# Two units of the third transform factor at once at a quad's end, and one tile for partial sums and output

## The chip, the cores and the metric

The kernel runs on one core of one Trainium2 chip. The metric is the device time of one execution in microseconds (us). The reports call the engines PE (TensorE matmul), PEld (TensorE weight load), DVE (VectorE), ACT (ScalarE), POOL (GpSimd) and SP (SyncE, which issues most DMAs here; "SPq" is its queue).

## The reference, cut to what matters

```python
# x: (8, 3008, 256), filt: (1505, 256), w_in: (256, 2048), w_out: (2048, 256), all float32 in effect
Y = np.fft.rfft(x, axis=1) * (filt_r + 1j * filt_i)[None]
x = np.fft.irfft(Y, n=3008, axis=1).reshape(24064, 256)
h = x @ w_in
g = np.where(h > 0.0, h, np.exp(np.minimum(h, 0.0)) - 1.0)
out = g @ w_out
```

A circular convolution along the sequence, by the frequency domain, and then a dense layer, an ELU and a second dense layer on every row.

## The kernel before

**Two parts side by side.** Each of the 8 batches goes through a transform in factors (3008 = 47 x 64) and then through the dense layers. While the dense layers of batch b - 1 run, pieces of the transform of batch b are placed between their steps. The work of a batch in the dense layers is 6 units (m = 0 to 5) of 512 rows (448 for m = 0) in four quads (q = 0 to 3, a quarter of the 2048 hidden columns each): 24 quads a batch, 192 in all. A *period* is 24 quads, and "quad 22" is the one with index 22 in it.

**A quad.** The two dense layers use a product scheme of seven multiplications in place of eight on blocks of 2 x 2. `up_steps` gives seven steps of the first layer (two matmuls each, `mm`, L583) into a PSUM bank taken from `banks`, with the sums on VectorE (L591), copies on ScalarE (L594) and the ELU on both (L600, L601, L605). `down_steps` gives seven steps of the second layer for the quad before it (L665), which add up in four banks `po0` to `po3` over four quads. The loop at the end (L1047 on) writes the order out by hand: U and D in the strings are the next up and down step, the first string of a quad, then the *places* 2 and 3 inside it, place 0 in the quad's middle, the second string, and place 1 at its end. A quad whose index is in `opens` starts with a down step: its strings are "DUUDUDDU" and "DUUDUD", else "UUDUDDU" and "DUUDUDD". `at(quad, place, ...)` puts a piece of other work there; every engine runs what it is given in this order, and the DMA queue of SP too.

**PSUM.** Eight banks: `po0` to `po3`, and four in the list `banks`, taken from its front and put back at its end. A quad's up steps hold two to three of these at a time.

**The pieces of the transform** of a batch, with their quads in the period: `a_unit` (first factor, L237; ends of quads 0, 3 and 4), `b_unit` (second factor, L388; ends of 6, 10, 14, 18), the products with the filter on VectorE, `bi_unit` (second factor back, L460, with ACT's copies at L463; ends of 9, 13, 17, 21), and `y_write` (L471), which writes a part of the DRAM tile `yd` right after. Each of these takes all four banks. Then the third factor, `n_unit` (L522 to L543), once for each unit m: `tn_read` (L483) loads its table, `y_read` (L494) loads rows of all of `yd` into a tile `t4` with two DMAs of 256 KB, one for each half of the partitions; 32 small matmuls of 64x64 shape (L535; 64 records in the trace) fill two banks, and ScalarE copies these to `y0` and `y1` (L542). `n_sums` (L545) makes the remaining operands of the up steps from them on VectorE, into `yb` and `yt`. Its places are written out at the end: `n_unit` stands in the middle (place 0) of quads 23, 25, 29, 32, 36 and 40, counted from the start of the period before the unit's own dense layers, whose first quad is 24; modulo 24 these are 23, 1, 5, 8, 12 and 16. `y_read` is placed two quads ahead in the middle of a quad, for m = 0 at the end of quad 21, behind the last `y_write`. Units 0 and 1 of batch 0 have another form, `n_whole`, with full-size matmuls.

**The end of a unit.** In the last quad's down steps ScalarE copies `po0` and `po1` to two tiles `k0` and `k1` of the pool `kp` (L670), VectorE joins them with `po2` and `po3` into `c` (L681, partly in `c_unit` in the next quad), and `o_unit` in the quad after that transposes `c` into `o`, a tile of a pool `op` of its own (L706), and issues 16 stores to the output (L715; 20 for m = 0). The last unit ends in `o_last`.

Pools give out buffers in turn; an instruction that writes to a buffer waits for the readers of its old content. SP's DMAs use eight semaphores in turn, and each waits for the DMA that used its semaphore before.

Of the kernel before, what the change touches and what calls it, by code (L numbers as in the profile page):

```python
# [11 lines left out]
FP32 = mybir.dt.float32  # L12
# [14 lines left out]
P = 128  # L27
# [106 lines left out]
def kernel(  # L134
# [371 lines left out]
    def n_whole(b, m):  # L506
        t, w, h = t4s.pop((b, m)), tns.pop((b, m)).rearrange("p i (k t) -> p i k t", k=2), half(m)
        rows = []
        for dh in range(2):
            y = yp.tile([P, 2, 256], FP32, tag="y%d" % dh, name="y%d" % dh)[:, :, 0:h]  # L510
            k, ps = bank("psn", (P, 2, 256))
            for q, i in enumerate(order(m)):
                nc.tensor.matmul(ps[:, :, ts(q, 64)], t[:, i - 4 * m, ds(dh * P, P)], w[:, i - 4 * m], start=True, stop=True)
            nc.scalar.activation(out=y, in_=ps[:, :, 0:h], func=AXT.Copy)
            banks.append(k)
            rows += [y[:, 0], y[:, 1]]
        b11, b12, b21, b22 = rows
        t = yp.tile([P, 2, 256], FP32, tag="yb", name="yb")[:, :, 0:h]
        t2 = yp.tile([P, 256], FP32, tag="yt", name="yt")[:, 0:h]
        ys[b, m] = {1: b11, 2: b21, 3: b22, 4: t[:, 1], 5: t[:, 0], 6: t2, 7: b12}  # L520

    def n_unit(b, m):  # L522
        if whole(b, m):
            return n_whole(b, m)
        t, w, h = t4s.pop((b, m)), tns.pop((b, m)), half(m)
        ps = [bank("psn", (P, 2, 256)) for _ in range(2)]
        for q, i in enumerate(order(m)):
            for dh in range(2):
                for c in range(2):
                    for (_, p), r in zip(ps, HALVES):  # L530
                        o = p[ts(c, 64), dh, ts(q, 64)]
                        if last(b, m):
                            o = p[ts(c, 64), dh, q:]
                            o = bass.AP(tensor=o.tensor, offset=o.offset, ap=[list(o.ap[0]), [131 - 2 * q, 2], [4, 32]])
                        nc.tensor.matmul(o, t[r, i - 4 * m, ds(dh * P + 64 * c, 64)],  # L535
                                         w[r, i - 4 * m, :], start=True, stop=True)
        even, odd, both = (yp.tile([P, 2, 256], FP32, tag=n, name=n)[:, :, 0:h] for n in ("y0", "y1", "yb"))
        t2 = yp.tile([P, 256], FP32, tag="yt", name="yt")[:, 0:h]
        ys[b, m] = {1: both[:, 0], 2: both[:, 1], 3: even[:, 1], 4: odd[:, 1], 5: odd[:, 0], 6: t2, 7: even[:, 0],
                    "even": even, "odd": odd, "both": both}  # L540
        for t, (k, p) in zip((even, odd), ps):
            nc.scalar.activation(out=t, in_=p[:, :, 0:h], func=AXT.Copy)  # L542
            banks.append(k)  # L543

    def n_sums(b, m, *parts):  # L545
        if whole(b, m):
            b11, b21, b22, t4, t1, t2, b12 = (ys[b, m][k] for k in range(1, 8))
            for o, x, y in ((t1, b12, b11), (b12, b22, b12), (t2, b22, t1), (t4, b21, t2)):
                nc.vector.tensor_tensor(out=o, in0=x, in1=y, op=ALU.subtract)
            return  # L550
        even, odd, both, t2 = (ys[b, m][k] for k in ("even", "odd", "both", 6))
        steps = ((both, odd, -0.5, even, ALU.add), (even[:, 1], odd[:, 1], 0.5, even[:, 1], ALU.add),
                 (t2, even[:, 1], 1.0, odd[:, 0], ALU.subtract), (even[:, 0], t2, 1.0, both[:, 0], ALU.subtract),
                 (odd[:, 1], both[:, 1], 1.0, t2, ALU.subtract))
        for i in parts or range(5):
            o, x, c, y, op = steps[i]
            if c == 1.0:
                nc.vector.tensor_tensor(out=o, in0=x, in1=y, op=op)
            else:
                nc.vector.scalar_tensor_tensor(out=o, in0=x, scalar=c, in1=y, op0=ALU.mult, op1=op)  # L560
# [92 lines left out]
    def down_steps(b, m, q):  # L653
        h = half(m)
        g = g_of.pop((b, m, q))
        if q == 0:
            po_of[b, m] = [psO.tile([P, 2, 256], FP32, tag="po%d" % i, name="po%d" % i) for i in range(4)]
        po = po_of[b, m]
        k = {}

        def step(n):
            i, u = PLACE[n]
            for a in range(2):

                nc.tensor.matmul(po[i][:, u, 0:h], w_out[q][:, COMBO[n], a, :], g[n][:, a, :],  # L665
                                 start=q == 0 and a == 0 and n in (1, 3, 6, 4), stop=True, skip_group_check=True)
            if q == 3 and n == 7:
                for i in range(2):
                    t = k[i] = kp.tile([P, 2, 256], FP32, tag="k%d" % i, name="k%d" % i)
                    nc.scalar.activation(out=t[:, :, 0:h], in_=po[i][:, :, 0:h], func=AXT.Copy)  # L670

        def tail():
            if q != 3:
                return
            p1, p5 = (k[0][:, u, 0:h] for u in range(2))
            p35, p7 = (k[1][:, u, 0:h] for u in range(2))
            c = kp.tile([P, 2, 512], FP32, tag="c", name="c")
            (c11, c12), (c21, c22) = ((c[:, i, 0:h], c[:, i, h:2 * h]) for i in range(2))

            def add(o, i0, i1):  # L680
                nc.vector.tensor_tensor(out=o, in0=i0, in1=i1, op=ALU.add)  # L681

            add(p35, p35, p5)
            add(c12, po[2][:, 1, 0:h], p1)
            add(c11, po[2][:, 0, 0:h], p1)
            rest = [(p7, p7, c12), (c21, po[3][:, 0, 0:h], p7), (c12, c12, p35), (c22, p7, p5)]
            cs_[b, m] = c, lambda i: [add(*r) for r in rest[i:i + 2]]

        return [(lambda n=n: step(n)) for n in DOWNS], tail


# [6 lines left out]
    def o_unit(b, m):  # L698
        c, join = cs_.pop((b, m))
        join(2)  # L700
        o = op.tile([P, 16, 2, 32], FP32, tag="o", name="o")
        if last(b, m):
            return o_last(b, m, c, o.rearrange("p (k f j) e s -> p k f (j e s)", k=2, f=2))
        n = 7 if m == 0 else 8
        for k in range(2):
            nc.vector.transpose(out=o.rearrange("p (j k) e s -> p j k e s", k=2)[:, 0:n, k],  # L706
                                in_=c[:, :, k * half(m):(k + 1) * half(m)].rearrange("p e (j s) -> p j e s", s=32))

        o = o.rearrange("p (u f k) e s -> p u f k (e s)", u=4, f=2)
        for k in range(2):  # L710
            for u, w, i in ((0, 3, 1), (3, 1, 0)) if m == 0 else ((0, 4, 4 * m),):
                for f in range(1 if i == 0 else 2):
                    n1 = N1 - i if f else i
                    for a in range(4):
                        nc.sync.dma_start(raw(out, b * N + n1 + 32 * N1 * k,  # L715
                                                   [[N1 * D, 32], [-D if f else D, w], [1, 64]], 64 * a),
                                               o[ts(a, 32), u:u + w, f, k])
# [121 lines left out]
    with tc.manual_schedule():  # L839


        with tc.tile_pool(name="boot", bufs=1) as bp:
# [24 lines left out]
            def places(m, e, c):  # L867
                wtmp.append((m.bitcast(U32), e.bitcast(U32), c[:, 0], c[:, 1]))

            def flat(t):  # L870
                return t.rearrange("p a b -> p (a b)")

            places(*(kp.tile([P, 512], FP32, tag=t, name=n) for t, n in (("k0", "wm"), ("k1", "we"))),
                   kp.tile([P, 2, 512], FP32, tag="c", name="wfl"))
            places(*(flat(sdp.tile([P, 2, D], FP32, tag="sd", name=n)) for n in ("wm", "we")),
                   t1p.tile([P, XC, D], FP32, tag="t1", name="wfl").rearrange("p (a b) d -> p a (b d)", a=2))
# [86 lines left out]
        yp = pool("yp", 2)  # L963
        gp = pool("gp", 2)
        ep = pool("ep", 2)
        op = pool("op", 1)
        n_unit(0, 0)
        n_sums(0, 0)

# [23 lines left out]
        for b in range(B):  # L993
            t = (b - 1) * PER
            if b > 0:
# [15 lines left out]
                for g in range(0, NG, 2):  # L1011
# [14 lines left out]
                    at(s + 3, 2, im_sums, b, g)  # L1026
                    at(s + 3, 1, bi_unit, b, g)
                    at(s + 3, 1, y_write, b, g)
            for m, s in enumerate((23, 25, 29, 32, 36, 40)):
                if b > 0 or m > 0:  # L1030
                    at(t + s - 2, 0, tn_read, b, m)
                    at(t + s - 2, 1 if m == 0 else 0, y_read, b, m)
                    if b == 0 and m == 1:
                        at(t + s, 1, n_unit, b, m)
                        at(t + s, 1, n_sums, b, m)
                    else:
                        at(t + s, 0, n_unit, b, m)
                        for place, *parts in (((t + s, 0), 0, 1, 2), ((t + s + 1, 2), 3, 4)) if m == 0 else (
                                ((t + s, 0), 0, 1), ((t + s, 1), 2, 3, 4)) if m < 3 else (((t + s + 2, 2),),):
                            at(*place, n_sums, b, m, *parts)  # L1040
                if b == 0 and m == 1:
                    at(1, 1, w_join, 13)
                at(t + PER + 4 * m + 5, 0, c_unit, b, m)
# [58 lines left out]
```

## Time and profile before

| | us |
|---|---|
| median of 3 runs | 2559.9 (2559.11 to 2561.76) |
| the profiled execution's own time | 2560.57 |
| its span, first to last instruction | 2558.6 |
| PE busy at L665 (down steps) | 1317.6 |
| PE busy at L583 (up steps), the five largest groups | 388.4 + 380.3 + 193.8 + 193.8 + 185.9 |
| PE busy at L535 (third factor) | 53.4 |
| DVE, ACT busy in all | 2066.1, 1544.9 |
| granted TensorE clock, mean | 0.997 |

The page gives busy times, the chain of work that ended last, and groups of instructions by source line. The timeline lists instructions in order of time, neighbours of one kind merged (start, length, engine, line, tiles, count; in brackets the engine's idle time ahead of them). Matmul records overlap: the start of the next one tells when the engine went on. The list of waits names who waited for whom, with the total, the count and the longest. The table by windows has, for each stretch, its length, the busy time and count of each engine, and at the end the granted clock, the DMA engines' share and GB/s.

### The profile page before, as it was taken

The numbers are of one execution on the slowest core, as the hardware profiler recorded it, in microseconds if no ns is written. First come the engines' busy times: TensorE is split into PE (matmuls) and PEld (weight loads), VectorE is DVE, ScalarE is ACT, GpSimd is POOL, SyncE is SP. The second block draws the span as 40 slices with busy tenths as digits, with TensorE's granted clock in tenths as the row PEclk, the third lists the DMA queues.
The fourth block names the chain that finished last, engine by engine and source line by source line (L and its number), as shares of the span: only waits on it lengthen the run. The fifth ranks groups of instructions, "written<-read, shape, count | busy, mean of one in ns | idle before, by whom it ended". The sixth has DMA issues, their size and how long they took to land.

```text
span 2558.6 us, 43997 instructions
## 1 busy us (share of the span) xinstructions
PE 2522.3 (99%) x16690; PEld 2164.8 (85%) x16690; DVE 2066.1 (81%) x3577; ACT 1544.9 (60%) x2716; POOL 160.2 (6%) x315
## 2 busy tenths in 40 slices
PE   6999999999999999999999999999999999999999
PEld 4788889888898888988889888888888888898888
DVE  6978887788878888788887888778897788876766
ACT  7765556655566565665566656565656655555555
POOL 5001000010000000000000000000100011000000
PEclk9999999999999999999999999999999999999999
DMA  9672213522133231433215231343213322110010
GB/s 281 178 189 65 62 39 81 130 67 69 44 102 100 67 69 40 121 82 72 57 44 150 64 80 36 77 122 81 60 41 85 84 63 69 36 46 18 19 28 17
DMA packets 228295, 200.62 MB, mean 78 GB/s; under 512 B 127174, under 2 KB 200406, under 8 KB 228084
## 3 DMA queue, kind: packets, MB, share of 16 engines
q1 hardware_dynamic: 213588, 166.93, 26.6%
q0 software_dynamic: 14000, 30.44, 4.3%
q8 instruction: 131, 2.15, 0.4%
q14 instruction: 80, 0.66, 0.1%
q10 hardware_dynamic: 496, 0.46, 0.1%
HBM read 125.86 MB, written 78.12 MB: 80 GB/s over the span
## 4 chain that ended last, share of the span: by engine, by line
PE 96%; DMA 2%; DVE 1%; ACT 0%; issue 0%; SPq 0%; DVEq 0%; ACTq 0%
PE po L665 45%; PE phs L583 25%; PE phd L583 13%; PE pha L583 6%; PE psn L535 2%; PE psa L237 2%; PE pf L388 1%; PE pv L460 1%; DMA xc<-in_x_dram 1%; DMA x<-in_x_dram 0%; PE po L333 0%; PE po L299 0%; DMA yd<-t 0%; PE psr L333 0%; DMA t<-yd 0%
## 5 line engine op out<-in xcount | busy, mean ns | idle before, releaser
L665 PE MATMUL po<-g,wo 128*128 128x256 f32 (+1 forms) x5376 | 1317.6, 377 | 0.0
L665 PEld LDWEIGHTS po<-g,wo 128*128 128x128 f32 x5376 | 1010.7, 190 | 165.8 <-issue 49.6
L594 ACT ACTIVATE g<-phs 128x512 f32<-128x512 f32 (+1 forms) x576 | 338.8, 588 | 737.1 <-PE phs L583 735.7
L601 ACT ACTIVATE e<-e 128x512 f32<-128x512 f32 (+1 forms) x768 | 477.2, 621 | 24.4
L605 DVE SCALAR_TENSOR_TENSOR g<-e,g 128x512 f32<-128x512 f32 (+1 forms) x576 | 387.3, 672 | 13.8 <-ACT e L601 13.4
L591 DVE TENSOR_TENSOR g<-phd,g 128x512 f32<-128x512 f32 (+1 forms) x384 | 258.7, 674 | 165.1 <-ACT e L601 107.7
L583 PE MATMUL phs<-y,wi 128*128 128x256 f32 (+1 forms) x1536 | 388.4, 375 | 0.0
L583 PE MATMUL phd<-y,wi 128*128 128x256 f32 (+1 forms) x1504 | 380.3, 375 | 0.0
L600 ACT ACTIVATE e<-g 128x512 f32<-128x512 f32 (+1 forms) x576 | 354.4, 615 | 34.1 <-DVE g L591 26.7
L583 PEld LDWEIGHTS phs<-y,wi 128*128 128x128 f32 x1536 | 291.9, 190 | 33.4 <-ACT g L594 0.2
L583 PEld LDWEIGHTS phd<-y,wi 128*128 128x128 f32 x1504 | 284.8, 190 | 35.1 <-DVE g L591 2.6
L605 DVE SCALAR_TENSOR_TENSOR g<-e,phs 128x512 f32<-128x512 f32 (+1 forms) x192 | 129.9, 677 | 115.5 <-ACT e L601 115.5
L583 PE MATMUL phs<-yt,wi 128*128 128x256 f32 (+1 forms) x768 | 193.8, 375 | 0.9 <-ACT g L594 0.9
L583 PE MATMUL phs<-yb,wi 128*128 128x256 f32 (+1 forms) x768 | 193.8, 375 | 0.6 <-ACT g L594 0.6
L583 PE MATMUL pha<-yb,wi 128*128 128x256 f32 (+1 forms) x736 | 185.9, 375 | 0.0
L600 ACT ACTIVATE e<-phs 128x512 f32<-128x512 f32 (+1 forms) x192 | 112.3, 585 | 111.9 <-PE phs L583 111.8
L591 DVE TENSOR_TENSOR g<-pha,g 128x512 f32<-128x512 f32 (+1 forms) x192 | 129.3, 673 | 45.5 <-PE pha L583 45.5
L583 PEld LDWEIGHTS phs<-yt,wi 128*128 128x128 f32 x768 | 145.7, 190 | 17.8 <-ACT g L594 1.2
L583 PEld LDWEIGHTS phs<-yb,wi 128*128 128x128 f32 x768 | 143.9, 190 | 19.3 <-ACT g L594 1.0
L327 POOL DMA_DIRECT2D fall<-fp x224 | 110.5, 501 | 721.9 <-DVE r L433 696.7
L583 PEld LDWEIGHTS pha<-yb,wi 128*128 128x128 f32 x736 | 139.8, 190 | 16.1
L642 DVE TENSOR_TENSOR g<-g,g 128x512 f32<-128x512 f32 (+1 forms) x192 | 130.7, 681 | 6.7
(170 smaller groups left out, 2066.3 us busy)
## 6 DMA issues: line engine op xcount, KB each, us to landing
yd<-t SPq DMA_DIRECT2D x127, 192.0 KB
t<-yd SPq DMA_DIRECT2D x92, 256.0 KB
z<-t SPq DMA_DIRECT2D x84, 256.0 KB
fall<-fp POOLq DMA_DIRECT2D x224, 96.0 KB, 3.0
t<-z SPq DMA_DIRECT2D x224, 96.0 KB
out_dram<-o SPq DMA_DIRECT2D x624, 32.0 KB
xc<-in_x_dram SPq DMA_DIRECT2D x84, 128.0 KB
xc<-in_x_dram SPq DMA_DIRECT2D x161, 64.0 KB
```

What stands on the lines that cost most here:

```text
L237: nc.tensor.matmul(p[o:o + 64, u, :], w[r, u, o:o + 64], src[r, u, :], start=True, stop=True)
L327: nc.gpsimd.dma_start(t[32 * a:32 * a + 24].rearrange("p c u d -> p (c u d)"), fp[g, a].rearrange("q c u d -> q (c u d)"))
L388: nc.tensor.matmul(pf[p][1][32 * a:32 * a + 32, js, :], fb[r, v, :], t2[r, js, a, :], start=True, stop=True, tile_position=(32 * p, 32 * a))
L535: nc.tensor.matmul(o, t[r, i - 4 * m, ds(dh * P + 64 * c, 64)], w[r, i - 4 * m, :], start=True, stop=True)
L583: nc.tensor.matmul(ps[:, a, 0:h], w_in[q][:, COMBO[n], a, :], y[n], start=start and a == 0, stop=True, skip_group_check=True)
L591: nc.vector.tensor_tensor(out=g[o], in0=i0, in1=i1, op=ALU.add)
L594: nc.scalar.activation(out=g[o], in_=i0, func=AXT.Copy)
L600: nc.scalar.activation(out=e, in_=src, func=AXT.Relu, scale=-1.0)
L601: nc.scalar.activation(out=e, in_=e, func=AXT.Exp, scale=-1.0)
L605: nc.vector.scalar_tensor_tensor(out=g[n], in0=es[n], scalar=1.0, in1=src, op0=ALU.subtract, op1=ALU.max)
L642: nc.vector.tensor_tensor(out=b12, in0=b22, in1=b12, op=ALU.subtract)
L665: nc.tensor.matmul(po[i][:, u, 0:h], w_out[q][:, COMBO[n], a, :], g[n][:, a, :], start=q == 0 and a == 0 and n in (1, 3, 6, 4), stop=True, ...
```

## The change

The split form of `n_unit` is called for two units in one go: `n_pair` runs units m and m + 1 one after the other at place 1, the end of a quad, in all four banks. The pairs (0, 1), (2, 3) and (4, 5) stand at the ends of quads 22, 29 and 36 (22, 5 and 12 modulo 24), and the quad after each is put in `opens`. For batch 0 the pair (0, 1) is left as it was. Table loads go two quads ahead of the pair, in the middle of the quad; the loads of units 0 and 1 at the end of quad 21, those of the others in the middle of quads 27 and 34. `n_sums` gets new places, and `yb` and `yt` are taken there and no longer in `n_unit`. `y0` and `y1` have three buffers in place of two. `k0` and `k1` become one tile with the tag `k`, and `o` takes the same place (same pool, same tag, one buffer); the pool `op` goes away.

```diff
-            y = yp.tile([P, 2, 256], FP32, tag="y%d" % dh, name="y%d" % dh)[:, :, 0:h]
+            y = yp.tile([P, 2, 256], FP32, tag="y%d" % dh, name="y%d" % dh, bufs=3)[:, :, 0:h]
...
+    def n_pair(b, m):
+        for k in (m, m + 1):
+            n_unit(b, k)
...
-        even, odd, both = (yp.tile([P, 2, 256], FP32, tag=n, name=n)[:, :, 0:h] for n in ("y0", "y1", "yb"))
-        t2 = yp.tile([P, 256], FP32, tag="yt", name="yt")[:, 0:h]
-        ys[b, m] = {1: both[:, 0], 2: both[:, 1], 3: even[:, 1], 4: odd[:, 1], 5: odd[:, 0], 6: t2, 7: even[:, 0],
-                    "even": even, "odd": odd, "both": both}
+        even, odd = (yp.tile([P, 2, 256], FP32, tag=n, name=n, bufs=3)[:, :, 0:h] for n in ("y0", "y1"))
+        ys[b, m] = {3: even[:, 1], 4: odd[:, 1], 5: odd[:, 0], 7: even[:, 0], "even": even, "odd": odd}
...
+        if "both" not in ys[b, m]:
+            h = half(m)
+            both = yp.tile([P, 2, 256], FP32, tag="yb", name="yb")[:, :, 0:h]
+            ys[b, m].update({"both": both, 1: both[:, 0], 2: both[:, 1],
+                             6: yp.tile([P, 256], FP32, tag="yt", name="yt")[:, 0:h]})
...
             if q == 3 and n == 7:
+                both = kp.tile([P, 2, 2, 256], FP32, tag="k", name="k")
                 for i in range(2):
-                    t = k[i] = kp.tile([P, 2, 256], FP32, tag="k%d" % i, name="k%d" % i)
+                    t = k[i] = both[:, i]
                     nc.scalar.activation(out=t[:, :, 0:h], in_=po[i][:, :, 0:h], func=AXT.Copy)
...
-        o = op.tile([P, 16, 2, 32], FP32, tag="o", name="o")
+        o = kp.tile([P, 2, 2, 256], FP32, tag="k", name="o").rearrange("p i u (j s) -> p (i u j) s", s=64).rearrange("p j (e s) -> p j e s", e=2)
...
-            for m, s in enumerate((23, 25, 29, 32, 36, 40)):
-                if b > 0 or m > 0:
+            for m, (s, sums) in enumerate(((22, (((23, 2), 0, 1, 2), ((23, 0), 3, 4))), (22, (((25, 0), 0, 1), ((25, 1), 2, 3, 4))),
+                                           (29, (((30, 2), 0, 1), ((30, 0), 2, 3, 4))), (29, (((34, 2),),)),
+                                           (36, (((38, 2),),)), (36, (((42, 2),),)))):
+                if b == 0 and m == 1:
+                    at(t + 23, 0, tn_read, b, m)
+                    at(t + 23, 0, y_read, b, m)
+                    at(t + 25, 1, n_unit, b, m)
+                    at(t + 25, 1, n_sums, b, m)
+                elif b > 0 or m > 0:
                     at(t + s - 2, 0, tn_read, b, m)
-                    at(t + s - 2, 1 if m == 0 else 0, y_read, b, m)
-                    if b == 0 and m == 1:
-                        at(t + s, 1, n_unit, b, m)
-                        at(t + s, 1, n_sums, b, m)
-                    else:
-                        at(t + s, 0, n_unit, b, m)
-                        for place, *parts in (((t + s, 0), 0, 1, 2), ((t + s + 1, 2), 3, 4)) if m == 0 else (
-                                ((t + s, 0), 0, 1), ((t + s, 1), 2, 3, 4)) if m < 3 else (((t + s + 2, 2),),):
-                            at(*place, n_sums, b, m, *parts)
+                    at(t + s - 1 if m < 2 else t + s - 2, 1 if m < 2 else 0, y_read, b, m)
+                    if m % 2 == 0:
+                        opens.add(t + s + 1)
+                        at(t + s, 1, n_pair, b, m)
+                    for (quad, place), *parts in sums:
+                        at(t + quad, place, n_sums, b, m, *parts)
```

More of the change, by code (lines that the diff above doesn't have):

```diff
@@ L871, in flat @@
                 return t.rearrange("p a b -> p (a b)")
-            places(*(kp.tile([P, 512], FP32, tag=t, name=n) for t, n in (("k0", "wm"), ("k1", "we"))),
+            k = kp.tile([P, 2, 2, 256], FP32, tag="k", name="wme").rearrange("p i u d -> p i (u d)")
+            places(k[:, 0], k[:, 1],
                    kp.tile([P, 2, 512], FP32, tag="c", name="wfl"))
@@ L965 @@
         ep = pool("ep", 2)
-        op = pool("op", 1)
         n_unit(0, 0)
```

## The prediction

> **What bounds the kernel now.** I read the page's busy times first, then the chain that ended last, then TensorE's timeline around one unit of the third factor, then the DMA queue's timeline and waits around its loads.
>
> ```profile
> span 2558.6 us, 43997 instructions
> PE 2522.3 (99%) x16690; PEld 2164.8 (85%) x16690; DVE 2066.1 (81%) x3577; ACT 1544.9 (60%) x2716; POOL 160.2 (6%) x315
> PE 96%; DMA 2%; DVE 1%; ACT 0%; issue 0%; SPq 0%; DVEq 0%; ACTq 0%
> ```
>
> TensorE is 96% of the chain. In the window from 300 to 2500 us its busy time is 2200.00 of 2200 us: it never waits there. What the change takes from TensorE's queue is therefore gained whole, and every wait that it adds to that queue is lost whole; waits of the other engines count only when they reach TensorE. An up or a down step (four records, because each product is two instructions and each instruction two records) takes 0.865 us at 256 columns and 0.757 at 224.
>
> TensorE's timeline around one unit now (start, length, records):
>
> ```profile
> 1036.15 0.92 PE L583 MATMUL phs<-y,wi 128*128 128x224 f32 x4
> 1037.00 1.16 PE L535 MATMUL psn<-tn,t 64*64 64x64 f32 x64
> 1038.10 1.02 PE L665 MATMUL po<-g,wo 128*128 128x224 f32 x4
> 1038.96 0.92 PE L583 MATMUL phd<-y,wi 128*128 128x224 f32 x4
> ```
>
> The step before it is over at 1036.15 + 0.757 = 1036.91; the step after it would have started at 1038.96 - 0.757 = 1038.20. The unit costs 1.29 us. Its 64 records: the last lasts 0.218 us and ends at 1038.16, so 63 starts lie in 0.94 us, 0.96 for all 64; the weight loads beside them span 1.02 us. I take 1.00 for the work and **0.29 us for going into the 64x64 shape and back** (0.27 to 0.33).
>
> The Trainium skill, "TensorEngine Tiling (Array Packing)", Key Properties, says that changing the tiling mode drains TensorE while tiles of one mode run independently; by that rule too a pair pays once, and the sum does not change.
>
> **The gain.** Batches 1 to 7 have six split units each, three pairs; batch 0 has two pairs (its units 0 and 1 stay as they are): 7 x 3 + 2 = 23 pairs, each saving one change of shape: 23 x 0.29 = **6.7 us** (6.2 to 7.6). If the second unit had to start afresh it would be 0; nothing in the rows separates two units in one shape, as 16 groups of the 64 follow one another at 0.06 us.
>
> **The loss: the first pair's data.** Pairs at quads 5 and 12 of a period have their loads issued in the middle of quads 3 and 10, over two quads (24 us) ahead: no wait. Units 0 and 1 of a batch need yd, whose last part leaves bi_unit at the end of quad 21. Now unit 0 runs in the middle of quad 23; after the change the pair stands at the end of quad 22. Batch 3:
>
> ```profile
> 990.79 1.14 PE L460 MATMUL pv<-zs,pairs 24*32 24x512 f32 x32
> 994.16 3.01 SPq L471 DMA_DIRECT2D yd<-t  x4
> 1000.64 1.16 SPq L494 DMA_DIRECT2D t<-yd  x2
> 1001.90 7.64 SPq L715 DMA_DIRECT2D out_dram<-o  x16
> 1004.06 1.03 PE L583 MATMUL phs<-yb,wi 128*128 128x256 f32 x4
> 1010.19 1.16 PE L535 MATMUL psn<-tn,t 64*64 64x64 f32 x64
> ```
>
> Quad 22 ends at 1004.06, where quad 23's first up step starts; with 0.09 us for the change of shape (as ahead of pv and psn) TensorE asks for unit 0's rows at 1004.15. Their two loads are issued at 1000.64, when the write of yd has landed: a lead of **3.51 us**, against 9.55 today. The change moves nothing of bi_unit, the write or this first load. In six of the seven batches the load is issued 9.72 to 9.90 us after pv starts; in batch 4 it is 11.25 (1300.38 to 1311.63), 1.4 us later.
>
> How long does such a load take? Later units show it: their two halves are followed by eight z reads, the queue hands out eight semaphores in turn, and so the eighth z read waits for the second half:
>
> ```profile
> 541.81 1.16 SPq L494 DMA_DIRECT2D t<-yd  x2
> 543.07 3.72 SPq L317 DMA_DIRECT2D t<-z  x8
> ```
>
> The list of the queue's waits names these:
>
> ```profile
> SPq L317 <- DMA t<-yd: 13.1, 21, 1.7
> ```
>
> The eighth issue itself takes 0.3 us, so it began at 546.49: landed 4.68 us after the first issue. Read so, eight loads took 4.40 to 4.83 us and three 6.3 to 6.9. From below: in batch 3 the data itself flows until about 1004.2, 3.6 us after issue, and the write's flow ends 0.5 us before the queue goes on, 4.1 in all. With 4.65, unit 0 waits 4.65 - 3.51 = 1.14 us.
>
> Unit 1's loads are now issued right behind (1.27 us later, the distance to the next issue above). If they take the same 4.65 us they land at 5.92; TensorE comes to them at 4.65 + 1.00 = 5.65: 0.27 us more. They share the DMA engines with unit 0's 0.52 MB: at 260 GB/s (270 and 246 in the two whole microseconds in which it flows) these take 2.0 us, 0.7 more than the head start of 1.27. Sum per batch 1.4 to 2.1 us; from below 0.9 (4.1 us for a load, no sharing), from above 3.7 (every load as slow as the slowest: 6.9 + 1.27 - 3.51 - 1.00). I take **1.8**, the middle of the typical rows with one slow load in seven. 7 x 1.8 + 1.4 for batch 4 = **14.0 us**. Behind the waiting matmuls stand all steps of quad 23, and behind these ACT's four copies; nothing overtakes.
>
> **The rest costs nothing.**
> - Banks at the quad's end: in batch 3's quad 12 the last up step ends at 1182.89 and VectorE's sum frees its bank at 1184.30, 1.4 us later; the pair's second unit starts at least one down step, 0.09 and 1.00 later (1.95). After the pair a down step (0.96) covers the copies: ACT's first pair of copies (1.08 us for two) ends 1.2 us into the second unit. Without that cover each bank late costs up to 0.6 us, one copy.
> - Output tile in the place of the partial sums: the copies of L670 now wait for the 16 stores of the unit before. In quad 22 these go behind unit 1's loads: 1003.2 to 1010.8 instead of 1001.90 to 1009.5, landed by 1014. The next copies start at 1023.69. Elsewhere the stores are issued by 1057.1, 1111.2 and 1160.7 and the copies come at 1071.07, 1127.14 and 1179.56: 12 us of margin or more.
> - Sums of the new units on VectorE: as many as before, none later than the quad before their first use. Third buffers for y0 and y1: their old users ended a quad earlier or more. At the end of the kernel o_last waits for the same sums as now.
>
> **Sum.** -6.7 + 14.0 = +7.3 us. The profiled execution took 2560.57 us (span 2558.6 and 2.0 around it), so 2567.9; the median shown is 0.7 lower: **2567**. A measurement of this kernel can tell some 0.2% (5.1 us) from no change: below 2554.8 is faster, above 2565.0 slower.
>
> **Rivals.**
> 1. *The loads come in time, or nearly (0.20).* For it: 3.51 us of lead is close to the 3.6 us at which the data ends, and unit 1's loads now take the place of the stores. Against it: none of the timed loads landed under 4.40. At a wait of 0 to 0.6 us a batch, and batch 4's 1.4: -5.3 to -1.1, 2554.6 to 2558.8. It is so if both units' loads land within 5.1 us of the first issue (3.51 + 1.00 + 0.6).
> 2. *The clock drops (0.15).* This kernel shows it once: TensorE stood idle from 83.49 to 85.68 us (2.19 us) and
>
> ```profile
> 86.00:87.00 1.00, 1.00 (x11) 1.00 (x10) 0.86 (x3) 0.97 (x3) 0.00 (x0) 0.90 1.01 335
> 87.00:88.00 1.00, 1.00 (x6) 1.00 (x6) 0.00 (x0) 1.00 (x2) 0.00 (x0) 0.50 1.01 361
> ```
>
> the granted clock (third figure from the right) was 0.50 until about 90.1, so 3.2 us at half speed, 1.6 us lost; after 1.66 us idle (117.8 to 119.46) it stayed at 1.00. If three of the seven waits set this off: 14.0 + 3 x 1.6 - 6.7 = +12, 2572; if all do, at waits of 2.5 us: 7 x (2.5 + 1.6) + 1.4 - 6.7 = +23, 2583. Against it: the wait is cut in two by a unit of matmuls. The Trainium skill, "TensorE: Matmul & The Clock Gate", Part 1, has the clock halved after at least one whole idle window of about 3.4 us; by that page no wait of mine would do it, but 2.19 us did here, so the row decides.
> 3. *A wait on the shared tile or a bank (0.05)*: one copy of 0.6 us in each of the 46 split units at worst, 28 - 6.7 = +21, 2581, without the first pair's wait; from the point where the stores land 10 us later than now. No row points there.
>
> The forecast has the remaining 0.60, 2562 to 2575. The range, 2556 to 2577, leaves out most of rival 1 and the end of rival 2. Faster 0.08 (rival 1 with hardly a wait), same 0.30 (0.12 from rival 1 and 0.18 from the forecast's end under 2565), slower 0.62.
>
> **What would show it.** Right: psn records at the end of quads 5 and 12 start 0.09 us behind the step before and the second 64 follow without a gap; at the end of quad 22 TensorE is idle some 1.1 us ahead of the first and 0.3 to 1.0 ahead of the second 64, put down to DMA t<-yd; no idle time at the copies of L670's successor. Wrong: no idle time in quad 22; idle time at the first up step of quads 23, 6 or 13 (banks); a granted clock under 1.00 after 300 us.

## The result, and the profile after

The changed kernel takes **2597.66 us** (median of 5, 2593.49 to 2604.33) against 2559.9 (median of 5, 2558.62 to 2568.51) on the same chip: ratio 1.0143, 95% interval 1.0125 to 1.0162. It is slower, as forecast, but far outside the predicted range (2556 to 2577). The profiled execution took 2593.49 us, 32.9 more than the one of before, where the sum was 7.3.

The page of the changed kernel, its first two lines, the chain by engine and one group of section 5 (busy, mean ns, then idle before and who ended it); "..." stands for lines left out:

```profile
span 2591.5 us, 44112 instructions
...
PE 2529.6 (98%) x16690; PEld 2167.4 (84%) x16690; DVE 2073.9 (80%) x3577; ACT 1544.0 (60%) x2716; POOL 159.4 (6%) x315
...
PE 84%; DVE 5%; DMA 4%; ACT 4%; issue 1%; SPq 1%; POOL 0%; ACTq 0%; DVEq 0%; POOLq 0%
...
L590 PE MATMUL phd<-y,wi 128*128 128x256 f32 (+1 forms) x1504 | 382.6, 377 | 12.8 <-DVE g L598 12.8
```

and from its list of waits:

```profile
PE phd L590 <- DVE g L598: 15.0, 23, 1.7
...
PE psn L539 <- DMA t<-yd: 10.2, 15, 0.9
```

TensorE does the same 16,690 matmuls, but the chain that ended last now runs more over VectorE, DMA and ScalarE: 84% instead of 96% is TensorE. The wait of psn for its rows was predicted. The other, of an up step (phd) for VectorE, was not, and it is the larger one in this list. Line numbers have moved by 4 to 8: up steps L583 to L590, VectorE's sums L591 to L598, ScalarE's copies L594 to L601, down steps L665 to L672, third factor L535 to L539, stores L715 to L723.

**Where the time came from.** Between 300 and 2500 us the records of after show TensorE idle for only 25.9 us. A better measure is the length of each quad, from one `pha` step to the next in TensorE's timeline, after minus before. Nearly all quads agree within 0.06 us; these do not (period 6 has the transform of batch 7 beside its dense layers, period 7, the last, has none):

```
quad of the period   1     5     6     7     8     12    13    14    16    22    23    sum
period 6           -1.29 +1.82 -0.87 +0.60 -0.34 +2.67 -0.72 +0.03 -0.43 +5.52 -2.15  +4.9
period 7           -1.28 +1.82 -0.86 -0.01 -1.28 +1.85 -0.86 +0.21 -1.29   -     -    -1.7
```

A unit that leaves a quad shortens it by 1.29 (quads 1, 8, 16 of period 7). A pair lengthens its quad by 2.26 and, if the next quad opens with a down step, moves 0.86 from that quad into its own; in period 7 the first two rows of a pair give 1.82 - 0.86 - 1.28 = -0.33, so **a pair gains 0.33 us**. The other pair of that period gives 1.85 - 0.86 + 0.21 - 1.29 = -0.09; the 0.21 in quad 14 goes in the runs below that do not open quad 13, so it belongs to the open quad and not to the pair. Seven periods are longer than these rows allow:

- quad 22: without a wait it would be +3.11 (-1.29 - 2.15 + 3.11 = -0.33). It is +5.73, 6.50, 7.36, 5.35, 5.67, 5.36 and 5.52: waits of 2.2 to 4.3, **19.7 us** in all;
- quads 7 and 8: 0.60 and 0.93 too long, **10.6 us** in all;
- quads 12 to 16: about 1.85 too long, **13.3 us** in all (0.2 of it in the last period).

19.7 + 10.6 + 13.3 - 23 x 0.33 = +36.0. The start of this execution was 3.3 us shorter (in the runs below it differs by -1.9 to +1.0), which leaves 32.7 of the 32.9. The median is 4.2 above the profiled run; the other executions were not traced.

**Quad 8.** TensorE in before and after (period 2), from the step ahead of the unit on:

```profile
814.49 1.03 PE L583 MATMUL phs<-y,wi 128*128 128x256 f32 x4
815.45 1.16 PE L535 MATMUL psn<-tn,t 64*64 64x64 f32 x64
816.54 1.13 PE L665 MATMUL po<-g,wo 128*128 128x256 f32 x4
817.51 1.03 PE L583 MATMUL phd<-y,wi 128*128 128x256 f32 x4
818.37 1.03 PE L583 MATMUL phs<-y,wi 128*128 128x256 f32 x4
819.24 1.03 PE L665 MATMUL po<-g,wo 128*128 128x256 f32 x4
820.10 1.03 PE L583 MATMUL phd<-y,wi 128*128 128x256 f32 x4
```

```profile
823.35 1.03 PE L590 MATMUL phs<-y,wi 128*128 128x256 f32 x4
824.21 1.03 PE L672 MATMUL po<-g,wo 128*128 128x256 f32 x4
825.08 1.03 PE L590 MATMUL phd<-y,wi 128*128 128x256 f32 x4
825.94 1.03 PE L590 MATMUL phs<-y,wi 128*128 128x256 f32 x4
826.80 1.03 PE L672 MATMUL po<-g,wo 128*128 128x256 f32 x4
828.49 1.13 PE L590 MATMUL phd<-y,wi 128*128 128x256 f32 x4 [0.66 <-DVE g L598]
829.46 1.89 PE L672 MATMUL po<-g,wo 128*128 128x256 f32 x8
```

VectorE at the same place, before and then after:

```profile
816.41 2.57 DVE L433 TENSOR_TENSOR r<-r,fall 128x512 f32<-128x512 f32 x4
818.91 0.68 DVE L591 TENSOR_TENSOR g<-phd,g 128x512 f32<-128x512 f32 x1
```

```profile
824.66 0.69 DVE L598 TENSOR_TENSOR g<-pha,g 128x512 f32<-128x512 f32 x1
825.27 2.57 DVE L433 TENSOR_TENSOR r<-r,fall 128x512 f32<-128x512 f32 x4
827.76 0.68 DVE L598 TENSOR_TENSOR g<-phd,g 128x512 f32<-128x512 f32 x1
```

The last `phd` step adds onto the bank of the `phd` step two up steps earlier, after VectorE has taken a sum from that bank (L598). Ahead of this sum stand four products of the filter (L433, `im_mult`, 2.57 us), placed in quads 8, 12 and 16. Before, the unit's 1.29 us stood in TensorE's queue just there: the first `phd` step started at 817.51, its sum was done at 818.91 + 0.68 = 819.59, and the last `phd` step came at 820.10, as the queue had it. Now the last `phd` step is due at 826.80 + 0.865 = 827.67, the sum is done at 827.76 + 0.68 = 828.44, and the step starts at 828.49. The next one follows 0.97 later (829.46) and not 0.865: 0.93 lost.

**Quad 22**, TensorE in after, period 2:

```profile
1013.23 1.03 PE L672 MATMUL po<-g,wo 128*128 128x256 f32 x4
1014.22 0.29 PE L539 MATMUL psn<-tn,t 64*64 64x64 f32 x2
1015.43 1.16 PE L539 MATMUL psn<-tn,t 64*64 64x64 f32 x62 [0.91 <-DMA t<-yd]
1016.84 0.29 PE L539 MATMUL psn<-tn,t 64*64 64x64 f32 x2 [0.25 <-issue]
1017.86 1.98 PE L539 MATMUL psn<-tn,t 64*64 64x64 f32 x62 [0.73 <-DMA t<-yd]
```

The SP queue, and one piece of the chain that ended last:

```profile
1004.20 3.03 SPq L471 DMA_DIRECT2D yd<-t  x4
1010.70 2.44 SPq L494 DMA_DIRECT2D t<-yd  x4
```

```profile
1012.55 5.17 DMA t<-yd
```

The four halves are issued from 1010.70 on. TensorE goes on with unit 0's second half at 1015.43, 4.73 us later; unit 1's second half is there at 1012.55 + 5.17 = 1017.72, 7.02 us after the first issue. The first matmul of a unit needs only one half, so each unit is cut into 2 and 62 records.

### The profile page after: what moved, and what is told of

It reads as the page before. It is cut to its first block, busy times and chain, and to the rows that moved or that the text cites. A ratio compares the mean times of both kernels' runs of the same rounds, so it can differ in the third digit from the quotient of the medians.

```text
span 2591.5 us, 44112 instructions
## 1 busy us (share of the span) xinstructions
PE 2529.6 (98%) x16690; PEld 2167.4 (84%) x16690; DVE 2073.9 (80%) x3577; ACT 1544.0 (60%) x2716; POOL 159.4 (6%) x315
## 3 DMA queue, kind: packets, MB, share of 16 engines
q8 instruction: 131, 2.15, 0.3%
## 4 chain that ended last, share of the span: by engine, by line
PE 84%; DVE 5%; DMA 4%; ACT 4%; issue 1%; SPq 1%; POOL 0%; ACTq 0%; DVEq 0%; POOLq 0%
PE po L672 39%; PE phs L590 22%; PE phd L590 11%; PE pha L590 6%; PE psn L539 2%; PE psa L237 2%; PE pv L460 1%; DVE g L598 1%; DMA t<-yd 1%; DMA yd<-t 1%; ACT e L607 1%; DVE g L612 1%; PE pf L388 1%; ACT e L608 1%; PE po L333 1%
## 5 line engine op out<-in xcount | busy, mean ns | idle before, releaser
L672 PE MATMUL po<-g,wo 128*128 128x256 f32 (+1 forms) x5376 | 1319.7, 377 | 0.0
L672 PEld LDWEIGHTS po<-g,wo 128*128 128x128 f32 x5376 | 1013.1, 190 | 165.2 <-issue 49.6
L601 ACT ACTIVATE g<-phs 128x512 f32<-128x512 f32 (+1 forms) x576 | 338.9, 588 | 759.2 <-PE phs L590 759.1
L598 DVE TENSOR_TENSOR g<-phd,g 128x512 f32<-128x512 f32 (+1 forms) x384 | 259.3, 675 | 260.1 <-ACT e L608 189.4
L590 PE MATMUL phd<-y,wi 128*128 128x256 f32 (+1 forms) x1504 | 382.6, 377 | 12.8 <-DVE g L598 12.8
L590 PE MATMUL phs<-y,wi 128*128 128x256 f32 (+1 forms) x1536 | 388.2, 375 | 2.9 <-ACT g L601 2.0
L590 PEld LDWEIGHTS phd<-y,wi 128*128 128x128 f32 x1504 | 283.2, 190 | 55.3 <-DVE g L598 24.2
L590 PEld LDWEIGHTS phs<-y,wi 128*128 128x128 f32 x1536 | 290.9, 190 | 38.4 <-ACT g L601 4.6
L590 PE MATMUL phs<-yb,wi 128*128 128x256 f32 (+1 forms) x768 | 193.9, 375 | 1.0 <-ACT g L601 1.0
L590 PE MATMUL phs<-yt,wi 128*128 128x256 f32 (+1 forms) x768 | 193.9, 375 | 0.9 <-ACT g L601 0.9
L598 DVE TENSOR_TENSOR g<-pha,g 128x512 f32<-128x512 f32 (+1 forms) x192 | 129.5, 674 | 77.2 <-PE pha L590 77.2
L590 PE MATMUL pha<-yb,wi 128*128 128x256 f32 (+1 forms) x736 | 185.9, 375 | 0.0
L590 PEld LDWEIGHTS phs<-yt,wi 128*128 128x128 f32 x768 | 145.7, 190 | 18.0 <-ACT g L601 1.5
L590 PEld LDWEIGHTS phs<-yb,wi 128*128 128x128 f32 x768 | 144.2, 190 | 19.7 <-ACT g L601 1.7
L590 PEld LDWEIGHTS pha<-yb,wi 128*128 128x128 f32 x736 | 139.8, 190 | 16.1
```

Of the source, the lines that this page charges most:

```text
L590: nc.tensor.matmul(ps[:, a, 0:h], w_in[q][:, COMBO[n], a, :], y[n], start=start and a == 0, stop=True, skip_group_check=True)
L598: nc.vector.tensor_tensor(out=g[o], in0=i0, in1=i1, op=ALU.add)
L601: nc.scalar.activation(out=g[o], in_=i0, func=AXT.Copy)
```

## The experiments

The theory after the first look: three separate waits, at quads 8, 12 and 16 (VectorE's products, uncovered: no unit runs on TensorE beside them any more), at quad 7 (a late copy on ScalarE) and at quad 22 (late rows). The rivals were that a pair itself, its banks, the shared tile or the clock costs the time. Each run is compared with before on its own chip; lengths of quads are those of its profiled execution, against before.

**Units moved out of quads 8, 12 and 16, nothing else** (before, units 3 to 5 in the middle of the next quad; no pair, no shared tile):

```diff
-                        at(t + s, 0, n_unit, b, m)
+                        at(t + s + (m > 2), 0, n_unit, b, m)
```

> The kernel before, with one thing moved: n_unit of units 3, 4 and 5 stands in the middle of quads 9, 13 and 17 and not of 8, 12 and 16. No pair, no new open quad, loads as before. Theory A: the units' 1.3 us in the middle of quads 8, 12 and 16 gave VectorE the time for its four products; without them each of these quads waits 0.85 to 0.93 us: 7 x 2.6 = 18 us slower than the kernel before. Rival B: the waits belong to the pairs (banks, copies, open quads); then this kernel takes as long as before, within 3 us.

2578.39 us, ratio 1.0066 (1.0051 to 1.0081). In the first seven periods quads 8, 12 and 16 lose 0.36, 0.44 and 0.44 instead of 1.29, while quads 9, 13 and 17 gain 1.29 each; in the last period all balance. That is 0.93 + 0.85 + 0.85 = 2.63 us a period and 18.3 in the span of the profiled execution (the ratio gives 17). The last `phd` step of quad 8 has the same wait as in after:

```profile
824.63 1.13 PE L583 MATMUL phd<-y,wi 128*128 128x256 f32 x4 [0.67 <-DVE g L591]
```

So this loss needs no pair. It comes from taking the unit away from where it stood.

**One of the four products to the quad's end** (after):

```diff
-                    early = 3 if g == 6 else 4
+                    early = 3
```

> The changed kernel, but in every group (and not in the last alone) only three of the four products of im_mult stand in the first half of a quad, the fourth goes to its end. Theory A: in quads 8, 12 and 16 TensorE's last up step (which adds onto the bank of step 7) waits for VectorE's sum of step 7, because four products of 0.64 us stand ahead of that sum and no unit's 1.3 us of matmuls stands any more between the quad's halves; one product less is 0.64 us, so nearly all of the 0.85 to 0.93 us by which each of these quads is long goes: 7 batches x 3 x 0.6 to 0.9 = 13 to 18 us faster than the changed kernel. Rival B: these quads are long because of the banks' new order or of ScalarE's copies after the pair; then the fourth product's place changes nothing, 0 us.

2585.9 us, ratio 1.0095 (1.008 to 1.011). Quads 8, 12 and 16 are each some 0.60 us shorter than in after, 12.7 us in all: one product on VectorE (2.57 / 4 = 0.64), just under the 13 to 18 that were expected.

**Two of the four to the end** (after, `early = 3 if g == 6 else 2`):

> The changed kernel, but only two of the four products of im_mult stand in the first half of quads 8, 12 and 16 (quad 20 keeps three), the other two go to the quad's end. Theory A (VectorE's sum of step 7 stands behind the products): one product less took 0.61 us from each of these quads and left 0.33, 0.25 and 0.25; two less take all of the 0.93, 0.85 and 0.85: 18 us faster than the changed kernel, unless the two at the end reach the first up steps of quads 9, 13 and 17. Rival: the 0.3 us left have another cause (ScalarE's chain from the first half to step 3); then this gives what one product less gave, 12 to 13 us.

2587.59 us, ratio 1.0109 (1.0095 to 1.0123). Quads 8, 12 and 16 now have no wait at all (-1.28, and +1.81 with the pair), but 0.49 us appears in each of quads 9 and 17: the moved products stand ahead of VectorE's sums there. The sum of quad 9's first `phd` step, in period 2, ends at 837.96 + 0.68 = 838.64, and the last `phd` step of quad 9 waits for it:

```profile
838.70 1.13 PE L590 MATMUL phd<-y,wi 128*128 128x256 f32 x4 [0.22 <-DVE g L598]
```

The cause is confirmed twice, and the repair is partial. The net gain in these quads is 10.2 us: 18.5, less 6.9 in quads 9 and 17 and less a single 1.4 in quad 9 of period 2, where `bi_unit` waited for GpSimd. In this execution the waits in quad 22 came to 2.8 us more than in after (+7.06, +7.04 and +6.67 in three periods), which hid part of it.

**Quad 6 not opened by a down step** (after):

```diff
-                        opens.add(t + s + 1)
+                        if m != 2:
+                            opens.add(t + s + 1)
```

> The changed kernel, but quad 6 (after the pair of units 2 and 3) is not put among the quads that start with a down step. Theory A: quad 7 is 0.60 us long because quad 6, now open, ends with one down step less between its last up step and b_unit of group 0, so that group's long chain (ACT, VectorE, ACT) reaches the copy of quad 7's third up step late; unopened, quad 7 loses 0.5 to 0.6 us in 7 batches: 3.5 to 4 us faster, if the first up step of quad 6 finds a bank. Rival B: it waits because the sums of unit 2 now stand in quad 6 on VectorE; then quad 7 stays as it is, and quad 6 may get longer by up to 0.9 us (bank), 0 to 6 us slower.

2592.33 us, ratio 1.0124 (1.0108 to 1.014). Quad 7 goes from +0.60 to 0.00 in every period, and quads 5 and 6 give the same sum as before the edit (+0.96 - 0.01 for +1.82 - 0.87): the first up steps find their banks free right behind a pair. In after, ScalarE's copy for quad 7 stands behind a copy for the second factor that waits for VectorE; this is ScalarE in after, period 2, and the up step that waits for it:

```profile
810.43 1.06 ACT L414 ACTIVATE r<-fall 32x1024 f32<-32x1024 f32 x1 [2.43 <-DVE r L407]
811.40 0.57 ACT L601 ACTIVATE g<-phs 128x512 f32<-128x512 f32 x1
```

```profile
812.02 1.13 PE L590 MATMUL phs<-y,wi 128*128 128x256 f32 x4 [0.33 <-ACT g L601]
```

My reading is that the down step spent at the start of quad 6 is missing later, where it covered this copy. What is shown is that opening quad 6 so costs the 0.6 us a period, and that the pair does not.

**No wait for the write** (after; units 0 and 1 of batches 1 to 7 read the rows of the batch before, so the loads wait for nothing):

```diff
-                                  yds[b][k.start + r:k.stop:2]...
+                                  (yds[b - 1] if b > 0 and m < 2 else yds[b])[k.start + r:k.stop:2]...
```

> The changed kernel, but units 0 and 1 of batches 1 to 7 load their rows from the previous batch's tile in DRAM, written long ago (so their results are those of other data): the loads no longer wait for the write of the last part. Theory A: all that quad 22 is long beyond the pair itself is the landing of these loads, with the clock's drop that follows in some batches; 2.2 to 4.3 us a batch, 19.7 us in the profiled run, go: 18 to 21 us faster than the changed kernel, and the granted clock keeps 1.00 after 300 us. Rival B: part of it is banks or ScalarE's copies at the quad's end; then quad 22 stays up to 1 us a batch longer than pair and shape cost, and the gain is 13 us or less.

2580.05 us, ratio 1.0074 (1.0057 to 1.009). Quad 22 is +3.26 to +3.96 long, 0.15 to 0.85 over 3.11, instead of +5.35 to +7.36: 16.7 us of TensorE's timeline are back, all in quad 22, a little under the expected 18 to 21. The loads, now issued beside the write, still end a little late; quad 22, period 2:

```profile
1012.63 1.15 PE L539 MATMUL psn<-tn,t 64*64 64x64 f32 x62 [0.29 <-DMA t<-yd]
```

**Rows loaded in two parts** (after; rows from 24 of the 32 groups in the middle of quad 21, the last 8 at its end behind the write):

```diff
+                    if m < 2:
+                        at(t + s - 1, 0, y_read, b, m, slice(0, 24))
+                        at(t + s - 1, 1, y_read, b, m, slice(24, K2))
```

> The changed kernel, but units 0 and 1 load their rows in two parts: 96 of the 128 partitions' rows (those written at the ends of quads 9, 13 and 17) in the middle of quad 21, the last quarter at its end, behind the last write of yd as before. Everything that is computed is the same. Theory A: what the pair in quad 22 waits for is the landing of these loads' data; four loads of 64 KB in place of four of 256 KB land some 4 us after the first issue in place of 6.9, within the 4.5 us that the second unit allows, so 15 to 20 us of the 19.7 go, and the clock's drops with them. Rival: the landing is a fixed delay of four loads in line and the size matters little; then 0 to 6 us go.

2589.34 us, ratio 1.0118 (1.0104 to 1.0132). Quad 22 is +4.09 to +5.90, some 1.1 us a period less than in after, 7.9 in all: neither the 15 to 20 of the theory nor the 0 to 6 of the rival. A quarter of the bytes does not take a quarter of the time. TensorE goes on with unit 1's second half 5.5 to 6.3 us after the first issue, where it was 6.7 to 7.2 in after; DMA issues are the same four, and the transfer runs at under half the rate. The table by windows (at the end of a line the clock, the share of the DMA engines and GB/s), first this kernel, then after, both while the rows flow:

```profile
1016.00:1017.00 1.00, 0.73 (x5) 0.26 (x3) 1.00 (x2) 0.82 (x2) 0.00 (x0) 1.00 0.30 95
1017.00:1018.00 1.00, 0.37 (x25) 0.40 (x29) 0.96 (x3) 0.80 (x2) 0.00 (x0) 1.00 0.55 119
1018.00:1019.00 1.00, 0.86 (x59) 0.75 (x53) 1.00 (x3) 0.19 (x1) 0.00 (x0) 1.00 0.52 104
```

```profile
1013.00:1014.00 1.00, 1.00 (x6) 0.76 (x4) 1.00 (x2) 0.97 (x2) 0.00 (x0) 1.00 0.95 254
1014.00:1015.00 1.00, 0.52 (x4) 0.19 (x2) 1.00 (x3) 0.80 (x3) 0.00 (x0) 1.00 1.07 242
```

**All three repairs** (the two-part load, two products early, and only the quad after pair (0, 1) opened):

> The changed kernel with the two parts of the load, two products in the first half, and quads 6 and 13 not open. If the three waits are all that the change brought beside the pairs' gain, all of 19.7 + 18 + 4 us go and the pairs' 23 x 0.33 us stay: 5 to 8 us faster than the kernel before (2552 to 2555 beside 2560). If waits mend by showing up elsewhere, it ends between the two kernels, 2565 to 2585.

2571.96 us, ratio 1.0051 (1.0039 to 1.0064). Still slower than before; waits mended in one place showed up in another, and the rows still came late. Its quads: 13.4 us of waits in quad 22 (about 1.5 a period, 4.5 in one, where the clock also fell), 6.9 in quads 9 and 17, 1.4 once in a quad 9 and 0.5 once in a quad 5, against 7.6 gained by the pairs: +14.6, where the span has +14.9.

**The shared tile alone** (before, `k0`, `k1` and `o` in one place, no pair; the third factor as it was):

```diff
+                both = kp.tile([P, 2, 2, 256], FP32, tag="k", name="k")
...
-        o = op.tile([P, 16, 2, 32], FP32, tag="o", name="o")
+        o = kp.tile([P, 2, 2, 256], FP32, tag="k", name="o").rearrange(...)
```

> The kernel before, with one part of the change alone: the two tiles of partial sums are one and the output tile takes its place (no pair, nothing moved). Theory A and the prediction: the stores land 10 us or more ahead of the next copies, so 0 us, within 3 us of before. Rival: ScalarE's copies wait for the stores in some units; then up to 0.6 us in each of 46 units, 5 to 28 us slower.

2559.33 us against 2559.54, ratio 0.9999 (0.999 to 1.0009). No quad differs by more than 0.06 us. The tile costs nothing.

**Another pair: units 1 and 2 only** (before with the shared tile and three buffers; in batches 1 to 7 units 1 and 2 at the end of quad 2, quad 3 opened, loads in the middle of quad 23; units 0, 3, 4 and 5 stay where they were):

```diff
+                elif b > 0 and m in (1, 2):
+                    at(t + 23, 0, tn_read, b, m)
+                    at(t + 23, 0, y_read, b, m)
+                    if m == 1:
+                        opens.add(t + 27)
+                        at(t + 26, 1, n_pair, b, m)
```

> The changed kernel's pair, shared tile and third buffers, but the pairs are others: in batches 1 to 7 only units 1 and 2 go together, at the end of quad 2 (quad 3 open, rows loaded two and a half quads ahead); units 0, 3, 4 and 5 stand in the middle of quads 23, 8, 12 and 16 as in the kernel before, so the quads with four products keep their cover and nothing waits for yd. Theory A: a pair by itself saves 0.33 us of change of shape; 7 x 0.33 = 2.3 us faster than the kernel before (2557 to 2558), and quads 1, 2 and 5 give -1.29, +0.96 net of the open quad, and -1.29 (quad 5: sum of the three -1.6 + the pair's 2.0 to 2.3). Rival: a pair costs something wherever it stands (banks, copies): same as before or slower.

2558.61 us against 2560.18, ratio 0.9992 (0.9983 to 1.0): 1.6 us faster, at the edge of what can be told: the interval reaches 1.0. Quads 1, 2, 3 and 5 give -1.29 + 3.00 - 0.76 - 1.28 = -0.33, with no wait elsewhere. Its median is the lowest of the versions here.

**The two late pairs, mended** (after; units 0 and 1 alone and where they were before, pairs (2, 3) and (4, 5) kept, no quad opened, `early = 2 if g == 2 else 3`):

> The changed kernel with units 0 and 1 single in the middle of quads 23 and 25 as before, pairs (2, 3) and (4, 5) at the ends of quads 5 and 12, no quad opened for them, and three of four products in the first half of quads 8, 16 and 20, two in quad 12. Theory A: the two pairs save 2 x 0.33 us a batch; what is left of the waits in quads 8 and 16 takes 0.33 + 0.25 us of that back in seven batches: 16 x 0.33 - 7 x 0.58 = 1.2 us faster than the kernel before, within 0.2% of it. Rival: waits move on to other quads, as two products late did in quads 9 and 17 (0.49 each): 3 to 8 us slower than before.

2559.83 us against 2560.18, ratio 0.9998 (0.9989 to 1.0007), no difference. What the pairs gain (16 x 0.33 = 5.3 us) goes into what is left of the waits: 0.33 in quad 8 and 0.24 in quad 16 in each of seven periods (4.0), and two single ones of 0.84 (quad 9, `bi_unit` waiting for GpSimd) and 0.51 (the first up step behind a pair, with no releaser in the trace).

## Why the prediction was wrong

1. **The failed step is the first one: "What the change takes from TensorE's queue is therefore gained whole"**, and its companion "The rest costs nothing", whose list has the banks at a pair's end, the tile and the sums, but nothing on what the units had covered in the quads they leave. In quads 8, 12 and 16 a unit's 1.29 us was also VectorE's time for four products. Taken away, 0.85 to 0.93 us of it came back as a wait: 2.63 us a period, 18.4 in seven, shown alone by the moved units (+18.3 in the span). With quad 7's 4.2 (0.60 x 7) and 1.3 in quads 12 to 14, most of which goes where quad 13 is not opened, this is the 23.9 us that the sum did not have. The forecast of 7.3, these 23.9, 5.7 more for the rows (point 3), 0.9 more gain (point 2) and the shorter start of 3.3 give 32.7 of the measured 32.9.

The profile of before had a row that showed it. The fourth call of `im_mult` in a period stands in quad 20, where no unit stands, and with three products instead of four. TensorE and VectorE in before, quad 20:

```profile
973.19 1.03 PE L583 MATMUL phd<-y,wi 128*128 128x256 f32 x4
974.05 1.03 PE L583 MATMUL phs<-y,wi 128*128 128x256 f32 x4
974.92 1.03 PE L665 MATMUL po<-g,wo 128*128 128x256 f32 x4
975.92 1.13 PE L583 MATMUL phd<-y,wi 128*128 128x256 f32 x4
976.89 1.89 PE L665 MATMUL po<-g,wo 128*128 128x256 f32 x8
```

```profile
973.38 1.89 DVE L433 TENSOR_TENSOR r<-r,fall 128x512 f32<-128x512 f32 x3
975.18 0.68 DVE L591 TENSOR_TENSOR g<-phd,g 128x512 f32<-128x512 f32 x1
```

The last `phd` step starts 1.00 us behind the down step instead of 0.865, as the sum ends (975.18 + 0.68), and its own 0.97 to the next start is longer too: 0.24 us lost, and quad 20 lasts 12.33 us where it lasts 12.09 in the last period. With a fourth product of 0.64 that is 0.88, the loss that quads 8, 12 and 16 then had. The sentence "it never waits there", taken from a busy time of 2200.00 of 2200 us, was wrong by this: the records of matmuls overlap, and a short wait shows in the starts alone.

2. **The gain**, 0.29 us a pair, 6.7 in all: right in kind, 0.33 and 7.6 measured (last period; quads 1 to 5 with the pair of units 1 and 2).

3. **The first pair's rows**, 1.8 us a period and 14.0 in all: the mechanism was right (the run with old rows), the size was 19.7. Unit 0's term held: 4.65 us from issue to landing was taken, 4.73 measured; 1.14 us of waiting was taken, and from 1014.25, behind the two records at 1014.22, to 1015.43 are 1.18. In the seven periods TensorE goes on 4.59 to 4.73 us after the first issue. (The rows of before were wider than the prediction read: of thirteen such loads that the wait of an eighth z read names, ten took 4.4 to 4.9 us, the others 5.2, 6.3 and 6.3.) Unit 1's did not: it was to land at 5.92 us after the first issue, by the lead of one issue plus an undisturbed load, or 0.7 later with the sharing, and landed 6.6 to 7.0 after it. The five quiet periods wait 2.24 to 2.62, 2.42 on average, over "1.4 to 2.1" and under the bound of 3.7. Four loads in line take longer each than two: in period 2 TensorE went on with unit 1's second half 5.31 us after that half's own issue (1012.55), with unit 0's 4.16 us after (1011.27). Only 1.8 was taken, the middle of the rows. Batch 4's extra 1.4 us did not come.

4. **The clock** (rival 2) came once in this execution, in period 2: granted 0.93, 0.50, 0.50, 0.50, 0.87 in the five us from 1017 on, some 1.7 us lost, where the rival had 1.6 for each drop. Without waiting (old rows) it stays at 1.00 after 300 us. In the other five variants with a pair in quad 22 it fell there once, twice or, with the two-part load alone, not at all. Another 1.0 us of quad 22 in period 1 goes largely into 0.53 ahead of unit 1's last five records, for which the trace gives no releaser. The same five records wait in period 1 of four other runs too (0.20, 0.83, 1.40 and 1.64 us), so it is no accident of one execution; its cause stays open.

5. **Rival 3 and the banks**: right as costing nothing. The shared tile alone changes no quad, and in after the first up steps behind a pair have no wait.

6. **Rival 1** did not occur: no load came in time.

7. **The range** was built from the costs that the text had named. 2577 left 10 us over the forecast, and the missing term alone was 24.

## What to carry to other kernels

A piece of work in the middle of the bound engine's queue is also time for the other engines: before it is moved, ask for each step behind it which sum, copy or load it waits for, and when that would be done without the piece. Measure a busy engine by the distance of starts from one repeat to the next, not by its busy time, and look for the one repeat without the piece: it has the price. Loads that are issued in line behind a write land one after another, so the last one counts, with the sharing, and not the first.

## What the runs showed of the hardware

- Two loads of 256 KB landed mostly 4.4 to 4.9 us after the first issue (ten of thirteen in before; the slowest took 6.3), four in line 6.6 to 7.0. Four of 64 KB, on 16 partitions each, took 6.0 in the version with all three repairs (period 2, issued from 1007.94 on, landed at 1013.93). The core's DMA traffic was 41 to 111 GB/s there, and 197 to 270 in after while the large ones on 64 partitions flowed. A smaller load that covers fewer partitions was hardly faster.
- The clock fell to half after 1.9 us of idle time in three pieces within 4 us, with matmuls between them. This is TensorE in after by windows (share busy, then at the end of a line clock, DMA share, GB/s):

```profile
1017.00:1018.00 1.00, 0.27 (x7) 0.17 (x9) 0.96 (x2) 0.59 (x2) 0.00 (x0) 0.93 0.42 82
1018.00:1019.00 1.00, 1.00 (x44) 1.00 (x47) 0.14 (x1) 0.00 (x0) 0.00 (x0) 0.50 0.17 31
```

  In period 0 nearly the same pattern (0.75, 0.48, 0.67 and 0.32 busy in the four us from 384 on, 1.8 idle) left it at 1.00. The Trainium skill, "TensorE: Matmul & The Clock Gate", Part 1, asks for at least one whole idle window of about 3.4 us and says that the windows run free of the program. The measured drop came with less idle time than that, 1.9 us in pieces, and here the measurement decides; that it comes in one period and not in another with nearly the same pattern agrees with windows that run free, and is not shown by it.
- The profiled execution of the variant with three products had +9.36 us in quad 22 of period 3, with the clock at half for some 6.8 us. Half of that, 3.4 us, is an estimate of what this one drop cost.
